# Loading an attention gradient's keys and query gradients already turned, by transposing DMAs

## The chip, the cores and the metric

The kernel runs on one core of a Trainium2 chip. The metric is device time in microseconds, as the median of several runs. The engines are called as the profile calls them: PE is TensorE (PEld its weight loads), DVE is VectorE, ACT is ScalarE, POOL is GpSimd, SP is SyncE, which issues the DMAs.

## The reference

Four residual layers over x of 2048 tokens by 512 features (bf16), each on a layer norm of x: attention, gated feed-forward, attention, gated feed-forward. The outputs are the result and, by `jax.vjp`, the gradients of x and of the five weights. The attention is linear, with 32 heads of 16:

```python
qkv = (x @ wqkv).reshape(B, S, 3, H, Dh)                     # q, k, v per head
phi = lambda t: jnp.where(t > 0, t + 1, jnp.exp(t)) + 1e-6
pq, pk = phi(q), phi(k)
kv = jnp.einsum("bhsd,bhse->bhde", pk, v)
z = jnp.einsum("bhsd->bhd", pk)
num = jnp.einsum("bhqd,bhde->bhqe", pq, kv)
den = jnp.einsum("bhqd,bhd->bhq", pq, z)[..., None] + 1e-6
o = num / den                                                # then @ wo
```

What matters here is the derivative of phi for the keys: for a positive key it is 1, for another exp(k), which is phi(k) - 1e-6. So the factor is min(pk - 1e-6, 1), and it can be made from the saved pk alone.

## The kernel before

Tokens are worked in 16 tiles of 128 (`NST`), features in four chunks of 128 (`NDC`). A forward pass over the four layers saves what the gradients need in DRAM (among it `pk`, the keys after phi, and `hT`, the normed input, turned). Then the gradient runs backwards over the layers: feed-forward 3, attention 2, feed-forward 1, attention 0. Weight gradients are sums over all tokens; they are computed by generators whose units (16 matmuls at line 1620, one PSUM bank, one evacuation) are put between the steps of other work: `next(fill)` issues one unit.

The gradient of an attention layer (class `ABwd`) has two parts. `first` computes the query gradients `dq` for all tokens, stores them in DRAM in two halves of 256 columns (`GW`), and computes the 512x512 product `GT`. `second`, the part that changes, runs over pairs of tiles (`NB2` = 2):

- `load(st)` loads a pair's `pk`, `dq`, `hT` and `h`, tokens on partitions; the first pair is loaded earlier, in `loaders`, into the tiles `pk_f`, `dq_f`, `hT_f`, `h_f`. All these DMAs are issued from SP, which issues one after another; a scheduler of the framework sets SP's order, while the orders of PE, DVE, ACT and POOL are as the program writes them (`manual_schedule`).
- `turn` transposes one tile's four chunks of `pk` and four of `dq` on PE into a PSUM bank (line 1869); ACT copies them to `pdT` (line 1870), and DVE makes the derivative factor `dphk` (line 1871).
- `keys` computes a pair's key gradients, turned: 16 matmuls into two banks (line 1881), and four DVE operations that add `dzc`, multiply by `dphk` and write `dkT` (line 1887).
- `finish` computes one tile's gradient of the normed input: 12 matmuls into one bank, four with `dq`, four with `pk`, the last four with `dkT` (line 1902). `LnAdd` then takes the layer norm's gradient: ACT makes a sum and, as a by-product that nobody reads, a copy into `dq_f` (line 1209); DVE makes a second sum and adds to x (lines 1210, 1211); POOL scales the two sums (line 1213). `end`, called a step later, makes the correction on ACT (line 1217) and adds it on POOL (line 1218). Its scratch is one of the first pair's tiles.
- `turn_keys` transposes four tiles of `dkT` in 32x32 blocks on DVE (line 989) and stores them; it runs for every second pair.

Before the loop stand the products of the layer (`ch_ps`), with two units of weight gradients between them. In the loop, a pair's `keys` come one pair ahead of its `finish`. PE's order in the loop for a pair is: turn, finish (even tile of the pair before), turn, keys, finish (odd tile of the pair before). PSUM has eight banks: "t", "g" and "u" with two each, "y" and "ln" with one each.

Of the kernel before, what the change touches and what calls it, by code (L numbers as in the profile page):

```python
# [9 lines left out]
BF16 = mybir.dt.bfloat16  # L10
F32 = mybir.dt.float32
ACT = mybir.ActivationFunctionType
ALU = mybir.AluOpType
# [5 lines left out]
D = 512  # L19
# [3 lines left out]
P = 128  # L23
NST = S // P
NDC = D // P
# [5 lines left out]
EPS = 1e-6  # L31
NB = 4
GW = 256
# [27 lines left out]
def ps_tile(k, which, shape, dt, name):  # L61
    return k.ps[which].tile(shape, dt, name=name, tag="ln_tp" if which == "ln" else f"{which}_ps")
# [318 lines left out]
def batch_rows(b, nb=NB):  # L381
    return slice(b * nb * P, (b + 1) * nb * P)


def dram_batch(ap2d, b, nb=NB):
    return ap2d[batch_rows(b, nb), :].rearrange("(n p) d -> p n d", p=P)
# [1262 lines left out]
class ABwd:  # L1649
# [161 lines left out]

    def loaders(self, fst):
        self.fst = {}
        self.fst["pk"] = fst.tile([P, 2, D], BF16, name="pk_f")
        self.fst["dq"] = fst.tile([P, 2, D], BF16, name="dq_f")
        self.fst["hT"] = fst.tile([P, 2, D], BF16, name="hT_f")
        self.fst["h"] = fst.tile([P, 2, D], BF16, name="h_f")
        for nm in ("pk", "dq", "hT", "h"):
            self.load_pair(nm, 0, self.fst[nm])

    def load_pair(self, nm, b, t):
        k, sv = self.k, self.k.sv[self.l]
        parts = [(t[:], sv[nm])]
        if nm == "dq":
            parts = [(t[:, :, g * GW:(g + 1) * GW], sv["dq"][g, :, :]) for g in range(D // GW)]
        for dst, src in parts:
            self.last_load = k.nc.sync.dma_start(out=dst, in_=dram_batch(src, b, 2)).ins

    def second(self, fill):
        k, l, small, ctx = self.k, self.l, self.small, self.ctx  # L1830
        nc, tc = k.nc, k.tc
        sv, NB2 = k.sv[l], 2
# [3 lines left out]
        Mv = late.tile([P, NDC, D], BF16, name="Mv")  # L1836
        with tc.tile_pool(name=f"ab_stg2{l}", bufs=2, reuse_waits="tile") as stg, \
# [7 lines left out]
            def load(st):  # L1845
                for nm in ("pk", "dq", "hT", "h"):
                    if st == 0:
                        cur[nm] = self.fst[nm]
                    else:
                        cur[nm] = stg.tile([P, NB2, D], BF16, name=f"{nm}_ld")  # L1850
                        self.load_pair(nm, st // NB2, cur[nm])
                with tc.issue_after(self.last_load):
                    if st == 6:
                        next(self.weights)
                    for b in (st - 2, st - 1):
                        if l == 2 and 0 <= b < NB:
                            k.load_a2(b)
                        if l == 0 and 0 <= b - 5 < NB:
                            k.load_h1(b - 5)
                return work.tile([P, NB2, NDC, P], BF16, name="dphk", bufs=1)  # L1860

            def turn(st, dphk):
                j = st % NB2
                T = dict(st=st, h=cur["h"][:, j, :])
                pdT = T["pdT"] = work.tile([P, 2, NDC, P], BF16, name="pdT", bufs=3)
                tps = ps_tile(k, "t", [P, 2, NDC, P], BF16, "T2_ps")
                for a, nm in enumerate(("pk", "dq")):
                    for c in range(NDC):
                        nc.tensor.transpose(tps[:, a, c, :], cur[nm][:, j, c * P:(c + 1) * P], k.ident[:])  # L1869
                nc.scalar.copy(pdT[:], tps[:])  # L1870
                nc.vector.tensor_scalar(dphk[:, j, :, :], pdT[:, 0, :, :], -EPS, 1.0, ALU.add, ALU.min)
                return T

            def keys(st, dphk):
                o = st % NB * P
                for half in range(2):
                    ps = ps_tile(k, "gu"[half], [P, 2, NB2 * P], F32, "dpk_ps")
                    for q in range(2):
                        c = 2 * half + q
                        for ic in range(NDC):  # L1880
                            nc.tensor.matmul(ps[:, q, :], lhsT=Nv[:, ic, c * P:(c + 1) * P],  # L1881
                                             rhs=cur["hT"][:, :, ic * P:(ic + 1) * P],
                                             start=(ic == 0), stop=(ic == NDC - 1))
                    for q in range(2):
                        c = 2 * half + q
                        tok = lambda t: t.rearrange("p (n t) -> p n t", n=NB2)
                        nc.vector.scalar_tensor_tensor(tok(dkT[:, c, o:o + NB2 * P]), tok(ps[:, q, :]), dzc[:, c:c + 1],
                                                       dphk[:, :, c, :], ALU.add, ALU.mult)

            def turn_keys(B):  # L1890
                for g in range(D // GW):
# [2 lines left out]
            def finish(T):  # L1894
                st = T["st"]
                dh_ps = ps_tile(k, ("y", "ln")[st % 2], [P, D], F32, "dh_ps")
                o = st % NB * P
                ops = [(T["pdT"][:, 1, c, :], k.wqkvT[:, c, :]) for c in range(NDC)]
                ops += [(T["pdT"][:, 0, c, :], Mv[:, c, :]) for c in range(NDC)]
                ops += [(dkT[:, c, o:o + P], k.wqkvT[:, NDC + c, :]) for c in range(NDC)]  # L1900
                for i, (lhsT, rhs) in enumerate(ops):
                    nc.tensor.matmul(dh_ps[:], lhsT=lhsT, rhs=rhs, start=(i == 0), stop=(i == len(ops) - 1))  # L1902
                spare = (self.fst[("pk", "hT")[st % 2]][:].rearrange("p n d -> p (n d)").bitcast(F32), self.fst["dq"][:, 0, :])
                ln = LnAdd(k, work, small, spare, dh_ps[:], T["h"], k.rstd[l][:, st:st + 1], k.xs[st])

                def end():
                    if self.out is None:
                        ln.end(k.xs[st][:])
                        return
                    out_t = outs[st // NB2 % 2]  # L1910
                    ln.end(out_t[:, st % NB2, :])
                    if st % NB2 == NB2 - 1:
                        nc.sync.dma_start(out=dram_batch(self.out, st // NB2, NB2), in_=out_t[:])
                return end

            dphk = load(0)
            Ts = [turn(j, dphk) for j in range(NB2)]
            dkv_ps = ps_tile(k, "g", [P, NDC, P], F32, "ch_ps")
            for c in range(NDC):
                cs = slice(c * P, (c + 1) * P)  # L1920
# [13 lines left out]
            for c in range(NDC):  # L1934
                ps = ps_tile(k, ("g", "y", "u", "ln")[c], [P, D], F32, "ch_ps")
                nc.tensor.matmul(ps[:], lhsT=dkvbdT[:, c, :], rhs=k.wqkvT[:, 2 * NDC + c, :], start=True, stop=True)
                evac_copy(k, Mv[:, c, :], ps[:], "vector" if c % 2 else "scalar")
            keys(0, dphk)
            prev, end = Ts, None
            for st in range(NB2, NST + NB2, NB2):  # L1940
                more, Ts = st < NST, []
                if more:
                    dphk = load(st)
                if not more:
                    end()
                    ends = [finish(T) for T in prev]
                    turn_keys(st // NB - 1)
                    for e in ends:
                        e()
                    break  # L1950
                for j in range(NB2):
                    Ts.append(turn(st + j, dphk))
                    if end is not None:
                        end()
                    if j:
                        keys(st, dphk)
                    end = finish(prev[j])
                if st % NB == NB2:
                    turn_keys(st // NB)
                prev = Ts  # L1960
# [10 lines left out]
def a_small_transposes(k, l, pool, GT, X_ld, dkvbdT):  # L1971
    nc = k.nc
    kvbdT = k.kv[l]["kvbdT"]
    T = {nm: pool.tile([P, NDC, w], BF16, name=nm) for nm, w in SMALL}
    jobs = [(T["G"][:, c, :], [GT[:, i, c * P:(c + 1) * P] for i in range(NDC)]) for c in range(NDC)]
    jobs += [(T["XT"][:, c, :], [X_ld[:, i, c * P:(c + 1) * P] for i in range(NDC)]) for c in range(NDC)]
    jobs += [(T["kvbd"][:].rearrange("p c f -> p (c f)"), [kvbdT[:, c, :] for c in range(NDC)]),
             (T["dkvbd"][:].rearrange("p c f -> p (c f)"), [dkvbdT[:, c, :] for c in range(NDC)])]
    for n, (dst, blocks) in enumerate(jobs):
        ps = ps_tile(k, "tg"[n % 2], [P, NDC, P], BF16, "fin_ps")  # L1980
        for i, b in enumerate(blocks):
            nc.tensor.transpose(ps[:, i, :], b, k.ident[:])
        evac_copy(k, dst, ps[:].rearrange("p c f -> p (c f)"), "vector" if n % 2 else "scalar")
    for nm, w in SMALL:
        nc.sync.dma_start(out=k.sv[l][nm].rearrange("(c p) j -> p c j", p=P), in_=T[nm][:])
# [58 lines left out]
```

## Time and profile before

| | |
|---|---|
| median of 3 runs | 1147.23 us (1147.04 to 1147.66) |
| the profiled execution | 1145.95 us, its span 1144.0 us |
| `second` of layer 2, first transpose to last `finish` | 599.4 to 669.9 us of the span |
| `second` of layer 0 | 935.9 to 1006.4 us of the span |
| DMA of the whole kernel | 258.18 MB, mean 226 GB/s |

The profile is one execution as the hardware profiler recorded it. Busy times are per engine; matmuls are pipelined and their ends modelled, so that the pitch from one to the next says more than the duration of one. Lines are those of the kernel file; a helper's operations all carry the helper's line.

### The profile page before, as it was taken

Reading aid. Unit: us, or ns where it says so; the run is one execution under the profiler, and the core shown is the slowest. Engines: PE = TensorE matmul, PEld = TensorE weight load, DVE = VectorE, ACT = ScalarE, POOL = GpSimd, SP = SyncE. Lnnn points to the kernel's source line nnn. Section 1 sums busy time; section 2 is a strip of 40 time slices with the busy share of each in tenths; the row PEclk is TensorE's granted clock in tenths of the full one; section 3 lists DMA queues with packets and bytes.
Section 4 is the critical chain, followed back from the end, with each engine's and each line's share of the span. In section 5 each row is a group of like instructions: output and inputs, shape, how many; then the busy total and the mean of one; then the engine's idle time right before and its main releaser. Section 6 shows DMA issues by size and latency. Waiting matters only on the chain. (4 is left out here: it accounts for less than half of the span.)

```text
span 1144.0 us, 21399 instructions
## 1 busy us (share of the span) xinstructions
PE 1122.8 (98%) x8026; PEld 698.8 (61%) x8026; DVE 745.5 (65%) x1311; ACT 552.9 (48%) x998; POOL 468.8 (41%) x627
## 2 busy tenths in 40 slices
PE   7999999999999999999999999999999999999998
PEld 4467777447777754445756656544447756665577
DVE  7787887888777667777966750067778947752221
ACT  4676666557676534445635651235546525630001
POOL 4738776435765446773102420048771103410000
PEclk9999999999999999999999999999999999999999
DMA  7945566534557677976899549787767886779775
GB/s 227 315 157 158 176 192 204 186 130 131 187 164 226 211 261 243 299 231 228 232 279 329 176 138 301 267 302 236 230 197 243 264 279 220 237 228 324 235 217 166
DMA packets 287145, 258.18 MB, mean 226 GB/s; under 512 B 29184, under 2 KB 263616, under 8 KB 287040
## 3 DMA queue, kind: packets, MB, share of 16 engines
q1 hardware_dynamic: 287040, 256.82, 70.4%
q8 instruction: 62, 1.02, 0.4%
q14 instruction: 43, 0.35, 0.1%
HBM read 136.25 MB, written 120.52 MB: 224 GB/s over the span
## 5 line engine op out<-in xcount | busy, mean ns | idle before, releaser
L1620 PE MATMUL p_ps<-p_set,p_a 128*128 128x384 bf16 (+2 forms) x1792 | 264.7, 303 | 1.3 <-DMA p_set<-sv_hdd 0.7
L1620 PEld LDWEIGHTS <-p_a 128*128 128x128 bf16 x1792 | 168.4, 95 | 84.3 <-PE p_ps L1620 1.0
L1329 POOL TENSOR_TENSOR dd<-dhb,ssd 128x512 bf16<-128x512 bf16 x84 | 96.9, 1157 | 110.6 <-ACT dhb L1327 108.0
L1328 DVE TENSOR_TENSOR dd<-dhh_ps,ssd 128x512 bf16<-128x512 f32 x85 | 57.2, 678 | 121.3 <-ACT dhb L1327 119.9
L1353 PE MATMUL dh_ps<-wuT,dd 128*128 128x512 bf16 (+1 forms) x340 | 128.9, 379 | 0.0
L1353 PE MATMUL dh_ps<-wgT,dd 128*128 128x512 bf16 (+1 forms) x340 | 128.8, 379 | 0.0
L1038 POOL TENSOR_TENSOR ssd_t<-hhT,oms 128x512 bf16<-128x512 bf16 (+1 forms) x92 | 99.8, 1091 | 67.2 <-DVE hhT L1037 42.6
L1353 PEld LDWEIGHTS <-dd 128*128 128x128 bf16 x680 | 66.4, 98 | 79.6
L1327 ACT CAST dhb<-dhh_ps 128x512 bf16<-128x512 f32 x84 | 48.7, 589 | 99.8 <-PE dhh_ps L1321 89.7
L1635 DVE TENSOR_TENSOR dw_stg<-p_ps,dw_stg 128x384 bf16<-128x384 f32 (+2 forms) x76 | 32.1, 437 | 99.0 <-PE p_ps L1620 96.2
L1019 PE MATMUL g_ps<-hT,wg 128*128 128x256 bf16 (+1 forms) x792 | 92.7, 260 | 1.6 <-ACT hT L376 0.9
L1019 PE MATMUL u_ps<-hT,wu 128*128 128x256 bf16 (+1 forms) x792 | 92.7, 261 | 0.8 <-DVE hhT L1037 0.8
L980 DVE STREAM_TRANSPOSE tr_stg<-dd 128x768 f32<-128x768 f32 (+1 forms) x62 | 86.6, 1436 | 1.1
L1037 DVE TENSOR_TENSOR hhT<-u_ps,ssd_t 128x512 bf16<-128x512 f32 (+1 forms) x92 | 58.0, 634 | 40.9 <-ACT ssd_t L1035 32.5
L1053 PE MATMUL y_ps<-wd,hhT 128*128 128x512 bf16 (+1 forms) x352 | 80.9, 379 | 0.1
L1321 PE MATMUL dhh_ps<-gT,wdT 128*128 128x512 bf16 x308 | 77.9, 379 | 1.2 <-DVE dd L1328 0.7
L1019 PEld LDWEIGHTS <-wg 128*128 128x128 bf16 x792 | 68.9, 98 | 16.0 <-issue 1.8
L1035 ACT ACTIVATE ssd_t<-g_ps 128x512 bf16<-128x512 f32 (+1 forms) x92 | 52.0, 565 | 50.9 <-PE g_ps L1019 33.6
L1019 PEld LDWEIGHTS <-wu 128*128 128x128 bf16 x792 | 70.6, 98 | 8.2 <-issue 1.2
L1637 ACT CAST dw_stg<-p_ps 128x384 bf16<-128x384 f32 (+2 forms) x76 | 28.1, 386 | 83.0 <-PE p_ps L1620 82.8
L1321 PEld LDWEIGHTS <-wdT 128*128 128x128 bf16 x352 | 33.9, 98 | 41.6 <-issue 3.8
L464 POOL TENSOR_TENSOR rstd_all<-rstd_all,neghalf 128x1 f32<-128x1 f32 x64 | 38.1, 596 | 47.5 <-DVE rstd_all L463 42.9
(276 smaller groups left out, 2085.9 us busy)
## 6 DMA issues: line engine op xcount, KB each, us to landing
sv_hdd<-tr_stg SPq DMA_DIRECT2D x72, 384.0 KB, 4.5
p_set<-sv_hdd SPq DMA_DIRECT2D x18, 1536.0 KB, 6.9
sv_ssd<-ssd_t SPq DMA_DIRECT2D x74, 256.0 KB, 2.4
ssd<-sv_ssd SPq DMA_DIRECT2D x23, 768.0 KB, 5.1
h_ld<-sv_h SPq DMA_DIRECT2D x30, 256.0 KB, 4.1
sv_hdl<-tr_stg SPq DMA_DIRECT2D x24, 256.0 KB, 4.7
p_a<-sv_h SPq DMA_DIRECT2D x12, 512.0 KB, 6.0
p_set<-sv_hdl SPq DMA_DIRECT2D x24, 256.0 KB, 5.3
```

The source lines that it names most:

```text
L980: nc.vector.transpose(t[:, :, 0:n * P].bitcast(F32).rearrange("p q (a j) -> p q a j", a=2 * n), src.rearrange("p c x -> p (c x)").bitcast( ...
L1019: nc.tensor.matmul(ps[:, ci * n:(ci + 1) * n], lhsT=w_sb[:, kc, (c0 + ci) * P:(c0 + ci + 1) * P], rhs=hT[:, kc, (st % 2) * P:(st % 2) * P ...
L1035: nc.scalar.activation(ssd[:, :, 0, :], gv, ACT.Sigmoid)
L1037: nc.vector.tensor_tensor(hh, uv, ssd[:, :, 0, :], ALU.mult)
L1038: nc.gpsimd.tensor_tensor(ssd[:, :, 1, :], hh, oms, ALU.mult)
L1053: nc.tensor.matmul(y_ps[:], lhsT=h[0:r, fc, off:off + P], rhs=k.wd[0:r, fc, :], start=(fc == 0), stop=(fc == NFC - 1))
L1321: nc.tensor.matmul(ps[:], lhsT=k.wdT[:, jc, u * P:(u + 1) * P], rhs=self.gT[B][:, jc, :], start=(jc == 0), stop=(jc == NDC - 1))
L1327: nc.scalar.copy(dhb[:], ps[:])
L1328: nc.vector.tensor_tensor(self.dd[ng][:, 0, c, :], ps[:], self.ssd[ng][:, c, 0, :], ALU.mult)
L1329: nc.gpsimd.tensor_tensor(self.dd[ng][:, 1, c, :], dhb[:], self.ssd[ng][:, c, 1, :], ALU.mult)
L1353: nc.tensor.matmul(self.acc[j][:], lhsT=dd[0:r, a, c, j * P:(j + 1) * P], rhs=w[0:r, u, :], start=(u == 0 and a == 0), stop=(u == NFC - 1 ...
L1620: nc.tensor.matmul(ps[:, 0:w], lhsT=lhs[:, s, ic * P:(ic + 1) * P], rhs=rhs, start=(s == 0), stop=(s == NST - 1))
```

## The change

`load_pair` loads `pk` and `dq` by `dma_start_transpose`: one DMA for a pair's keys (256 tokens by 512 columns), two for its query gradients (256 by 256 each). They arrive with features on partitions, as `[P, NDC, 256]`, in three buffers instead of two. `turn` is gone, with its transposes, `pdT` and PSUM bank; `finish` takes its weights from the loaded tiles. `dphk` is made once for a pair, by POOL, at the head of `keys`. The by-product of line 1209 goes to a PSUM tile of bank "t" instead of `dq_f`, and the correction's scratch for tile 0 is `hT_f`. One more unit of weight gradients stands ahead of the layer's products (the total is the same), and the transposes at the end of the layer take their banks in the other order.

```diff
     def loaders(self, fst):
         self.fst = {}
-        self.fst["pk"] = fst.tile([P, 2, D], BF16, name="pk_f")
-        self.fst["dq"] = fst.tile([P, 2, D], BF16, name="dq_f")
+        for nm in ("pk", "dq"):
+            self.fst[nm] = fst.tile([P, NDC, 2 * P], BF16, name=f"{nm}T_f")
...
     def load_pair(self, nm, b, t):
         k, sv = self.k, self.k.sv[self.l]
-        parts = [(t[:], sv[nm])]
-        if nm == "dq":
-            parts = [(t[:, :, g * GW:(g + 1) * GW], sv["dq"][g, :, :]) for g in range(D // GW)]
-        for dst, src in parts:
-            self.last_load = k.nc.sync.dma_start(out=dst, in_=dram_batch(src, b, 2)).ins
+        pair = batch_rows(b, 2)
+        if nm == "pk":
+            ins = k.nc.sync.dma_start_transpose(out=t[:], in_=sv["pk"][pair, :])
+        elif nm == "dq":
+            for g in range(D // GW):
+                n = GW // P
+                ins = k.nc.sync.dma_start_transpose(out=t[:, g * n:(g + 1) * n, :], in_=sv["dq"][g, pair, :])
+        else:
+            ins = k.nc.sync.dma_start(out=t[:], in_=dram_batch(sv[nm], b, 2))
+        self.last_load = ins.ins
...
-                        cur[nm] = stg.tile([P, NB2, D], BF16, name=f"{nm}_ld")
+                        if nm in ("pk", "dq"):
+                            cur[nm] = stg.tile([P, NDC, NB2 * P], BF16, name=f"{nm}T_ld", bufs=3)
+                        else:
+                            cur[nm] = stg.tile([P, NB2, D], BF16, name=f"{nm}_ld")
...
-            def turn(st, dphk):
-                j = st % NB2
-                T = dict(st=st, h=cur["h"][:, j, :])
-                pdT = T["pdT"] = work.tile([P, 2, NDC, P], BF16, name="pdT", bufs=3)
-                tps = ps_tile(k, "t", [P, 2, NDC, P], BF16, "T2_ps")
-                for a, nm in enumerate(("pk", "dq")):
-                    for c in range(NDC):
-                        nc.tensor.transpose(tps[:, a, c, :], cur[nm][:, j, c * P:(c + 1) * P], k.ident[:])
-                nc.scalar.copy(pdT[:], tps[:])
-                nc.vector.tensor_scalar(dphk[:, j, :, :], pdT[:, 0, :, :], -EPS, 1.0, ALU.add, ALU.min)
-                return T
...
-            def keys(st, dphk):
+            def keys(st):
                 o = st % NB * P
+                dphk = work.tile([P, NDC, NB2 * P], BF16, name="dphk", bufs=1)
+                nc.gpsimd.tensor_scalar(dphk[:], cur["pk"][:], -EPS, 1.0, ALU.add, ALU.min)
...
-                ops = [(T["pdT"][:, 1, c, :], k.wqkvT[:, c, :]) for c in range(NDC)]
-                ops += [(T["pdT"][:, 0, c, :], Mv[:, c, :]) for c in range(NDC)]
+                ops = [(T["dq"][:, c, :], k.wqkvT[:, c, :]) for c in range(NDC)]
+                ops += [(T["pk"][:, c, :], Mv[:, c, :]) for c in range(NDC)]
...
-                spare = (self.fst[("pk", "hT")[st % 2]][:].rearrange("p n d -> p (n d)").bitcast(F32), self.fst["dq"][:, 0, :])
+                r = self.fst["hT" if st == 0 or st % 2 else "pk"][:].rearrange("p n d -> p (n d)").bitcast(F32)
+                spare = (r, ps_tile(k, "t", [P, D], F32, "t_junk")[:])
...
-            dphk = load(0)
-            Ts = [turn(j, dphk) for j in range(NB2)]
+            prev = load(0)
+            next(fill)
...
                 for j in range(NB2):
-                    Ts.append(turn(st + j, dphk))
                     if end is not None:
                         end()
                     if j:
-                        keys(st, dphk)
+                        keys(st)
                     end = finish(prev[j])
```

More of the change, by code (lines that the diff above doesn't have):

```diff
@@ L1859, in load @@
                             k.load_h1(b - 5)
-                return work.tile([P, NB2, NDC, P], BF16, name="dphk", bufs=1)
-            def turn(st, dphk):
-                j = st % NB2
-                T = dict(st=st, h=cur["h"][:, j, :])
-                pdT = T["pdT"] = work.tile([P, 2, NDC, P], BF16, name="pdT", bufs=3)
-                tps = ps_tile(k, "t", [P, 2, NDC, P], BF16, "T2_ps")
-                for a, nm in enumerate(("pk", "dq")):
-                    for c in range(NDC):
-                        nc.tensor.transpose(tps[:, a, c, :], cur[nm][:, j, c * P:(c + 1) * P], k.ident[:])
-                nc.scalar.copy(pdT[:], tps[:])
-                nc.vector.tensor_scalar(dphk[:, j, :, :], pdT[:, 0, :, :], -EPS, 1.0, ALU.add, ALU.min)
-                return T
-            def keys(st, dphk):
+                return [dict(st=st + j, h=cur["h"][:, j, :], pk=cur["pk"][:, :, j * P:(j + 1) * P],
+                             dq=cur["dq"][:, :, j * P:(j + 1) * P]) for j in range(NB2)]
+            def keys(st):
                 o = st % NB * P
+                dphk = work.tile([P, NDC, NB2 * P], BF16, name="dphk", bufs=1)
+                nc.gpsimd.tensor_scalar(dphk[:], cur["pk"][:], -EPS, 1.0, ALU.add, ALU.min)
                 for half in range(2):
@@ L1885, in keys @@
                         c = 2 * half + q
-                        tok = lambda t: t.rearrange("p (n t) -> p n t", n=NB2)
-                        nc.vector.scalar_tensor_tensor(tok(dkT[:, c, o:o + NB2 * P]), tok(ps[:, q, :]), dzc[:, c:c + 1],
-                                                       dphk[:, :, c, :], ALU.add, ALU.mult)
+                        nc.vector.scalar_tensor_tensor(dkT[:, c, o:o + NB2 * P], ps[:, q, :], dzc[:, c:c + 1],
+                                                       dphk[:, c, :], ALU.add, ALU.mult)
             def turn_keys(B):
@@ L1937, in second @@
                 evac_copy(k, Mv[:, c, :], ps[:], "vector" if c % 2 else "scalar")
-            keys(0, dphk)
-            prev, end = Ts, None
+            keys(0)
+            end = None
             for st in range(NB2, NST + NB2, NB2):
[L1941 to L1944, printed above, removed]
+                if st < NST:
+                    Ts = load(st)
+                else:
                     end()
@@ L1979, in a_small_transposes @@
     for n, (dst, blocks) in enumerate(jobs):
-        ps = ps_tile(k, "tg"[n % 2], [P, NDC, P], BF16, "fin_ps")
+        ps = ps_tile(k, "gt"[n % 2], [P, NDC, P], BF16, "fin_ps")
         for i, b in enumerate(blocks):
```

## The prediction

> **What bounds the kernel now.** First the page's busy table, then the two stages that the change touches (function `second`, once per attention layer, found by the first and last starts of lines 1869 and 1902), by the view of windows.
>
> ```profile
> PE 1122.8 (98%) x8026; PEld 698.8 (61%) x8026; DVE 745.5 (65%) x1311; ACT 552.9 (48%) x998; POOL 468.8 (41%) x627
> 599.40:669.90 70.50, 70.50 (x517) 43.67 (x516) 48.26 (x106) 41.03 (x67) 23.10 (x43) 1.00 0.68 216
> 935.90:1006.40 70.50, 70.50 (x520) 43.67 (x518) 49.36 (x108) 40.27 (x65) 23.15 (x44) 1.00 0.70 219
> ```
>
> Columns of the last two: window, its length, busy of PE, PEld, DVE, ACT, POOL, granted clock, DMA share, GB/s. TensorE is never idle in either 70.5 us, at full clock. The chain that ended last, in order of time, shows how one pair of tiles is paced (start, duration, what):
>
> ```profile
> 973.43 1.75 PE dpk_ps L1881 x16
> 975.18 2.59 PE dh_ps L1902 x12
> 977.77 0.45 PE T_ps L1869 x8
> 978.22 2.59 PE dh_ps L1902 x12
> 980.80 0.45 PE T_ps L1869 x8
> 981.25 1.75 PE dpk_ps L1881 x16
> ```
>
> A pair takes 7.82 us of pure TensorE: two `finish` (2.59 each), one `keys` (1.75), two turns (0.45 each). So the stage is TensorE's, and what leaves TensorE shortens it only if no chain through other engines is as long. The timeline shows that chain (start, duration, engine, line, names):
>
> ```profile
> 980.90 0.69 ACT L1209 ACTIVATE dq_f<-dh_ps,rstd_all 128x512 bf16<-128x512 f32 x1 [0.27 <-PE dh_ps L1902]
> 981.49 0.19 ACT L1209 ACTIVATION_READ_ACCUMULATOR dq_f<-dh_ps,rstd_all 128x1 f32 x1
> 981.77 0.75 DVE L1210 SCALAR_TENSOR_TENSOR junk<-dh_ps,rstd_all,h_ld 128x512 bf16<-128x512 f32 x1 [1.40 <-issue]
> 982.61 0.19 POOL L1213 TENSOR_SCALAR ab<-c 128x1 f32<-128x1 f32 x1 [0.48 <-DVE junk L1210]
> 982.84 0.81 ACT L1217 ACTIVATE pk_f<-h_ld,ab,ab 128x512 f32<-128x512 bf16 x1 [0.25 <-POOL ab L1213]
> 983.11 0.28 DVE L1871 TENSOR_SCALAR dphk<-pdT 128x512 bf16<-128x512 bf16 x1
> 983.50 1.66 DVE L1887 SCALAR_TENSOR_TENSOR dkT<-dpk_ps,dzc,dphk 128x256 bf16<-128x256 f32 x4
> 983.74 1.27 POOL L1218 TENSOR_TENSOR out_t<-x,pk_f 128x512 bf16<-128x512 f32 x1 [0.93 <-ACT pk_f L1217]
> ```
>
> The even tile's layer-norm end runs ACT, DVE, POOL, ACT, POOL and is finished at 985.01. Today nothing on TensorE needs it: `dphk` is made on DVE (983.11), `dkT` starts at 983.50. That POOL takes its instructions strictly in turn can be seen a tile later, in POOL's own timeline:
>
> ```profile
> 988.53 1.28 POOL L1218 TENSOR_TENSOR out_t<-x,hT_f 128x512 bf16<-128x512 f32 x1 [0.93 <-ACT hT_f L1217]
> 989.78 0.19 POOL L1213 TENSOR_SCALAR ab<-c 128x1 f32<-128x1 f32 x1
> 990.94 0.19 POOL L1213 TENSOR_SCALAR ab<-c 128x1 f32<-128x1 f32 x1 [0.96 <-DVE junk L1210]
> ```
>
> The first L1213 of the even tile had its operand at 989.50 (ACT's read of the sum ended) and started only when the odd tile's add was over.
>
> **Removed from TensorE.** 16 tiles x 8 transposes x 2 layers = 256. Eight take 0.446 us (980.80 to 981.25), so 14.3 us, all on the path. ACT loses 32 evacuations (L1870, 1.00 us each), DVE 32 `dphk` (L1871, 0.28): neither set the pace. Alone this gives 6.93 us a pair.
>
> **The step that decides: `dphk` on POOL.** POOL executes in order. In the changed program its order for a pair is: two L1213 and the add L1218 of the odd tile before, two L1213 and L1218 of the even tile, then `dphk`. So `dphk`, which needs only the loaded keys, waits for the even tile's add, and the four `dkT` operations (L1887, now 1886) wait for `dphk`; behind these on DVE stand the odd tile's L1210 and L1211, and TensorE's next `finish` needs `dkT` for its last four matmuls. That `finish` feeds the next L1209: a ring through all four engines. One lap, from the end of `dkT`:
> - DVE does the odd tile's L1210 at once (+0.05). From the start of an L1210 to the end of its L1217 the rows above give 983.65 - 981.77 = 1.88 us. ACT holds the next even tile's L1209 behind that L1217, and L1209 to L1210 is 0.87, so the even L1210 starts at 0.05 + 1.88 + 0.87 = 2.80. TensorE is not last there: its fourth `dkT` matmul ends at about 0.3, ACT could start at 0.6.
> - L1210's start to L1218's end: 985.01 - 981.77 = 3.24, now 6.04.
> - `dphk`, 128x1024 on POOL: no such row, but the groups by line have its half, a two-operation tensor_scalar:
>
> ```profile
> L224 POOL TENSOR_SCALAR out_t<-x 128x512 bf16<-128x512 f32 x2 | 1.2, 620 | 2.1 <-DVE x L1055 2.1
> ```
>
>   Twice that less one start of about 0.09 is 1.15, now 7.19. Bounds: 0.62 (no growth with width) and 2.12 (the 128x1024 tensor_tensor of L891).
> - handover and four `dkT`: 0.05 + 1.66 = 1.71, the lap is **8.90**.
> - Every second pair the two key transposes (L989, 2.09 us) stand on DVE behind the odd L1211 (which ends at 1.48): the even L1210 starts at 3.57 and the lap is **9.67**.
>
> The mean is 9.29 against TensorE's 6.93: TensorE would stand idle 2.4 us a pair, where today it is never idle.
>
> **Sum for a layer**, from the first `finish` to the last: the first lap starts free, with `dkT` ready at 2.59 + 1.13 (end of `finish` to L1210) + 3.24 + 1.15 + 1.71 = 9.8; six laps follow, three of each kind, 55.7; then the last `finish` waits for its PSUM bank (L1211 of the tile two before, 1.5 after `dkT`) and takes 2.59. That is 69.6. Today: 7 x 7.82 + 2 x 2.59 = 59.9. Less the first pair's 16 transposes (0.89): +8.8 a layer, **+17.6** for two. Each 0.1 us in a lap is worth 7 x 2 x 0.1 = 1.4, so `dphk` at its bounds gives +10 or +31.
>
> **The transposing loads.** No run here shows one. Each pair asks for three (keys 256 KB, query gradients 2 x 128 KB), three buffers deep instead of two; needed about two laps after issue. Lower bound: as the plain loads, which land in 4.5 us (keys) and 4.4 (gradients): hidden, 0; a gain is excluded, as no engine waits for a load in these stages today. For the work: queue 1 shows 287040 packets in 70.4% of 16 engines' span, 44.9 ns each. Plain, a pair has 256 key rows and 512 half rows, 768 packets; if a turned load moves 128 columns of a row at a time, 2048: 3.6 us more a pair on 16 engines. The stage's DMA work, 0.68 and 0.70 of 70.5, grows from 48 and 49 us to 73 and 74, in a stage that by the ring lasts 79: hidden, narrowly. I take 0, the same queue and bytes, and keep the upper bound as a rival. [...]
>
> **At nothing.** One unit of 16 filler matmuls (2.64 us) goes from the stage's end to its head: TensorE does it either way. It covers the first pair's loads, as do the chain products: `dqT_f` is first used some 12 us after the transposes of today (599.4); without that cover up to its 4.4 us. The sum's copy (L1209) goes to PSUM: between 0.59 (L1327, a cast of the same size) and 0.81 (L1217) for 0.69, which over 14 laps is 2 us either way. On SP the issues of a pair (980.66 to 988.47) take 3.3 us, the three now turned 1.5 of them; even at three times that SP is done in 6.3, below the lap. There the later loads change places (hT first, `h` behind the keys of the next pair but one, which wait for a free buffer); all are issued a lap or more ahead, and if one is late `finish` or L1210 waits for it. POOL's eight `dphk` a layer delay only L1213 and L1218, which the lap counts. The stage after gets its `x` as late as the ring ends, no more.
>
> The profiled execution took 1145.95 us (span 1144.0 and 1.95 around it); the median is 1147.23, 1.28 above. 1145.95 + 17.6 + 1.28 = **1164.8**.
>
> **Rivals.**
> 1. *The ring does not bind* (faster). For: POOL is only a third busy in the stage (23.1 of 70.5), and the transposes are on the path. The point from which it decides is a mean lap of 8.0 (9.29 less 8.8 / 7), where gain and ring cancel; at 6.93 or less the whole gain is left: 1147.2 - 14.3 = 1133. It could come if `dphk` and the handovers cost almost nothing. Against: `dphk` at 0.3 still leaves 8.4, and the other terms are rows of operations that stay, in the same order. Chance 0.08.
> 2. *The turned loads set the pace.* If only one is under way at a time, each at its plain landing time, a pair takes 4.5 + 2 x 4.4 = 13.3 us, more than the lap; seven pairs from the stage's start and some 9 us of work behind the last make 102 instead of 70.5: 2 x 31.5 more, 1210. For: by the packets above the DMA work has only 5 us of room a stage, and a turned packet may take longer than a plain one. Against: plain loads of this queue overlap freely, and the lap itself leaves each load some 18 us. Chance 0.17. [...]
> 3. *No difference*: laps near 8.0, gain and ring cancel, 1147. Chance 0.03.
>
> **How the numbers follow.** Forecast 0.72. The range 1153 to 1202 takes the forecast with `dphk` at either bound (1157 to 1179), 4 us below for handovers that are quicker than read, and on the other side part of rival 2, loads that lengthen each stage by up to 18 us more (1164.8 + 2 x 18.6); it leaves out rival 1, no difference, and the rest of rival 2. A measurement of this kernel can tell some 0.2% (2.3 us) from none: faster 0.08, same 0.03, slower 0.89.
>
> **What would show it.** In the changed trace: the stages last about 79 us, not 70.5; TensorE idles in them before the last four matmuls of the even `finish`, released by L1886; DVE waits at L1886 for POOL's `dphk`; POOL's row shows `dphk` at 1.15 directly behind L1218; starts of `dphk` 8.9 and 9.7 us apart in turn. I am wrong if TensorE stays full and a pair takes 6.93, or if POOL's `dphk` or TensorE's first group of `finish` waits for DMA, which is rival 2.

## The result, and the profile after

The changed kernel takes 1198.13 us (median of 5 runs, 1195.62 to 1200.46) against 1147.23 for the kernel before on the same chip (5 runs, 1147.04 to 1148.17): a ratio of 1.0443, interval 1.043 to 1.0455. That is 50.9 us slower, where 17.6 were forecast. The profiled execution took 1198.13 us, its span 1196.2.

The page's busy table, and the two stages by the view of windows. The columns are those of before: window, length, busy PE, PEld, DVE, ACT, POOL, granted clock, DMA share, GB/s. Each window starts with the moved filler unit (2.64 us) and ends with the last `finish`.

```profile
PE 1130.2 (94%) x7770; PEld 688.3 (58%) x7770; DVE 737.5 (62%) x1279; ACT 521.8 (44%) x966; POOL 527.5 (44%) x643
599.51:697.00 97.49, 77.23 (x415) 40.68 (x414) 44.17 (x90) 25.92 (x52) 48.52 (x50) 0.91 0.59 158
962.06:1060.63 98.57, 78.38 (x423) 41.37 (x422) 46.05 (x94) 25.27 (x50) 48.49 (x50) 0.91 0.66 163
```

PE has the 256 instructions fewer that were announced, yet it is idle for 20 us in each stage. POOL's busy time has doubled, from 23.1 to 48.5. The page's groups name the two waits, one behind the other:

```profile
L1901 PE MATMUL dh_ps<-wqkvT,dkT 128*128 128x512 bf16 x128 | 42.4, 427 | 39.6 <-DVE dkT L1886 39.6
L1886 DVE SCALAR_TENSOR_TENSOR dkT<-dpk_ps,dzc,dphk 128x256 bf16<-128x256 f32 x64 | 26.6, 477 | 78.1 <-POOL dphk L1875 77.8
```

PE waits 39.6 us for `dkT`; DVE, before `dkT`, waits 77.8 us for POOL's `dphk`. One lap of the ring in the timeline (start, duration, engine, line, names):

```profile
653.61 3.63 POOL L1875 TENSOR_SCALAR dphk<-pkT_ld 128x1024 bf16<-128x1024 bf16 x1
...
657.27 1.66 DVE L1886 SCALAR_TENSOR_TENSOR dkT<-dpk_ps,dzc,dphk 128x256 bf16<-128x256 f32 x4 [5.56 <-POOL dphk L1875]
...
657.81 1.89 PE L1901 MATMUL dh_ps<-wqkvT,dkT 128*128 128x512 bf16 x4 [4.16 <-DVE dkT L1886]
...
658.84 0.74 DVE L1210 SCALAR_TENSOR_TENSOR junk<-dh_ps,rstd_all,h_ld 128x512 bf16<-128x512 f32 x1
...
659.90 0.81 ACT L1217 ACTIVATE hT_f<-h_ld,ab,ab 128x512 f32<-128x512 bf16 x1 [7.07 <-POOL ab L1213]
660.62 0.64 ACT L1209 ACTIVATE t_junk<-dh_ps,rstd_all 128x512 f32<-128x512 f32 x1
...
661.42 0.75 DVE L1210 SCALAR_TENSOR_TENSOR junk<-dh_ps,rstd_all,h_ld 128x512 bf16<-128x512 f32 x1 [1.16 <-ACT t_junk L1209]
...
662.49 0.81 ACT L1217 ACTIVATE pkT_f<-h_ld,ab,ab 128x512 f32<-128x512 bf16 x1 [1.10 <-POOL ab L1213]
...
663.38 1.26 POOL L1218 TENSOR_TENSOR x<-x,pkT_f 128x512 f32<-128x512 f32 x1 [0.93 <-ACT pkT_f L1217]
...
664.73 3.63 POOL L1875 TENSOR_SCALAR dphk<-pkT_ld 128x1024 bf16<-128x1024 bf16 x1
```

This is the ring that the prediction drew, operation for operation: `dphk`, `dkT`, the odd tile's L1210 and L1217, the even tile's L1209, L1210, L1217 and L1218, then the next `dphk`. Each starts within 0.1 us of the end of the one before it, but for two small steps between them: ACT's read of its sum behind L1209, and POOL's L1213 between an L1210 and its L1217. The starts of `dphk` in this stage lie 11.13 and 11.87 us apart in turn (641.73, 653.61, 664.73, 676.59, 687.71). The new thing is the first line: `dphk` takes 3.63 us. The lines of one source show that it always does (number, then min/median/max in ns), and how the turned loads stand:

```profile
L1875 POOL TENSOR_SCALAR dphk<-pkT_ld x14: 3626/3626/3643, 618.7 to 1051.3; 128x1024 bf16<-128x1024 bf16 x14
L1826 SPq DMA_TRANSPOSE pkT_ld<-sv_pk x14: 1226/1252/7255, 598.7 to 1028.2; - x14
L1830 SPq DMA_TRANSPOSE dqT_ld<-sv_dq x28: 1188/1264/2622, 602.1 to 1030.7; - x28
```

A turned load keeps SP for about 1.25 us (the median; the longest took 7.3). No engine waits for one in the loop. Only ahead of the loop does POOL's first `dphk` of a layer wait for a DMA: 6.0 us for the first pair's keys (`pkT_f`, at 952.8, layer 0), and 5.7 us in layer 2, which the profile puts down to the store of `dq`; nothing was late for either.

Where the 52.2 us of span (1196.2 less 1144.0) are: from the first chain product (L1922) to the start of the last four `dkT` matmuls a stage took 68.75 and 68.74 us before and takes 93.99 and 95.07 now, which is +51.6; the first pairs' transposes are gone (-1.8); and PE waits 3.1 us instead of 0.7 for `p_set` at 726.92, behind layer 2's stage (+2.4).

### The profile page after: what moved, and what is told of

The parts are those of the page before. It is cut to its first block, busy times and chain, and to the rows that moved or that the text cites. A ratio compares the mean times of both kernels' runs of the same rounds, so it can differ in the third digit from the quotient of the medians.

```text
span 1196.2 us, 20805 instructions
## 1 busy us (share of the span) xinstructions
PE 1130.2 (94%) x7770; PEld 688.3 (58%) x7770; DVE 737.5 (62%) x1279; ACT 521.8 (44%) x966; POOL 527.5 (44%) x643
## 5 line engine op out<-in xcount | busy, mean ns | idle before, releaser
L1901 PE MATMUL dh_ps<-wqkvT,dkT 128*128 128x512 bf16 x128 | 42.4, 427 | 39.6 <-DVE dkT L1886 39.6
L1886 DVE SCALAR_TENSOR_TENSOR dkT<-dpk_ps,dzc,dphk 128x256 bf16<-128x256 f32 x64 | 26.6, 477 | 78.1 <-POOL dphk L1875 77.8
```

## The experiments

The theory (A, where the expectations use letters): the ring sets the pace, because `dphk` is queued on POOL behind the even tile's add, and its length is the operation's own. Rivals: the turned loads share in the loss; `dphk` is slow only beside other work; the moved unit costs something. The runs are counted here in the order in which they are told. Intervals below are those of the ratio to the kernel before, run on the same chip (medians 1147.13 to 1147.86).

**1. The factor on DVE, nothing else undone.**

```diff
-                nc.gpsimd.tensor_scalar(dphk[:], cur["pk"][:], -EPS, 1.0, ALU.add, ALU.min)
+                nc.vector.tensor_scalar(dphk[:], cur["pk"][:], -EPS, 1.0, ALU.add, ALU.min)
```

> The changed kernel with its derivative factor on DVE (same place in the program, same 128x1024 operation), so that only the turned loads are left of the change. Theory (the ring through POOL's dphk costs all, the turned loads nothing): the ring is broken, a pair takes TensorE's 6.93 us, 1147.2 - 14.3 = 1133, TensorE without idle time in the two stages; dphk about 0.49 us on DVE (L662 of before, 128x1024). Rival (the turned loads pace the stages): TensorE or DVE waits for pkT_ld or dqT_ld, the time stays above 1147. Second rival (turned loads cost other transfers their time): stages at 6.93 a pair, but stalls elsewhere, 1135 to 1147.

Measured: 1147.16 us (1142.14 to 1149.24, 12 runs), ratio 0.9995 (0.9983 to 1.0007). All of the loss is gone, and with it the waits for `dkT`; but the 1133 that the theory gave is missed, and of the gain nothing is left. PE's waits and the place of the longest in PE's timeline:

```profile
PE dpk_ps L1881 <- DMA hT_ld<-sv_hT: 5.1, 1, 5.1
PE p_ps L1620 <- DMA p_set<-sv_hdd: 3.1, 2, 2.7
```
```profile
990.74 3.57 PE L1881 MATMUL dpk_ps<-hT_ld,X_Nv 128*128 128x256 bf16 x16 [5.09 <-DMA hT_ld<-sv_hT]
994.11 1.83 PE L1901 MATMUL dh_ps<-wqkvT,dqT_ld 128*128 128x512 bf16 x4
```

In layer 0's stage PE stands 5.09 us for a plainly loaded tile, `hT`, and the matmuls behind it run at half pace (16 in 3.57 us, 1.91 elsewhere). SP's own timeline shows what went just ahead of it:

```profile
985.26 1.28 SPq L1830 DMA_TRANSPOSE dqT_ld<-sv_dq  x1
986.59 0.57 SPq L1832 DMA_DIRECT2D hT_ld<-sv_hT  x1
987.26 1.36 SPq L1826 DMA_TRANSPOSE pkT_ld<-sv_pk  x1
988.67 2.57 SPq L1830 DMA_TRANSPOSE dqT_ld<-sv_dq  x2
```

SP issues almost without a pause, and `hT` was issued at 986.59 behind the turned loads; 4.1 us later it is there. In layer 2, where no load is late, the stage is 62.49 us in the measure above: the 68.75 of before less 14 tiles x 0.446. So the saving on PE is real. The accounts of this span (1145.1): -14.3 as forecast, +8.8 in layer 0's stage (71.30 instead of 62.5), +3.9 between the stages, +2.4 ahead of the first (1.7 of it before any line that was changed), +0.4 behind.

**2. The same place on POOL, a cheap pair of operators.** The minimum is left out.

```diff
-                nc.gpsimd.tensor_scalar(dphk[:], cur["pk"][:], -EPS, 1.0, ALU.add, ALU.min)
+                nc.gpsimd.tensor_scalar(dphk[:], cur["pk"][:], 1.0, 0.0, ALU.mult, ALU.add)
```

> The changed kernel with POOL's operation of the same size and place, but a multiply by 1 and an add of 0 in place of the add and the min; it leaves the minimum out, so the factor is wrong where a key is over 1. Theory A (the minimum is what makes POOL's operation take 3.63 us instead of 1.15): it takes about 1.15, laps of 8.9 and 9.7 us, and the time is the forecast's sum, 1165. Theory B (bf16 source, or the width): it stays at 3.6 us, and the time at 1198. Between the two, each 0.1 us of the operation should be worth 14 laps x 0.1 = 1.4 us.

Measured: 1159.51 us (1158.18 to 1160.72), ratio 1.0099 (1.0083 to 1.0115). The line's durations, and PE's wait:

```profile
L1875 POOL TENSOR_SCALAR dphk<-pkT_ld x14: 1044/1044/1047, 619.1 to 1018.0; 128x1024 bf16<-128x1024 bf16 x14
```
```profile
PE dh_ps L1901 <- DVE dkT L1886: 12.6, 11, 1.5
```

Same ring, same place, 1.044 us instead of 3.626: laps of 8.42 and 9.15, and 38.6 us less. That is 15.0 us for each us of `dphk`; the prediction had 14. It is 5.5 us below the 1165 that was expected: `dphk` is 0.1 us shorter than the forecast's 1.15, and the laps are another 0.4 shorter than its sum.

**3. What the operation costs by itself.** POOL operations on their own data, behind the end of the changed kernel; the whole program's time (1234.15 us, one run) is of no use here.

```diff
+        for _ in range(2):
+            g(ob[:], sb[:], -EPS, 1.0, ALU.add, ALU.min)
+            g(ob[:, 0:D], sb[:, 0:D], -EPS, 1.0, ALU.add, ALU.min)
+            g(ob[:, 0:D], sf[:, 0:D], -EPS, 1.0, ALU.add, ALU.min)
...
+            g(ob[:], sb[:], 1.0, 0.0, ALU.mult, ALU.add)
...
+            g(ob[:], sb[:], -EPS, 1.0, ALU.add, ALU.add)
+            g(ob[:], sb[:], -EPS, 1.0, ALU.add, ALU.mult)
...
+            g(ob[:], sb[:], 1.0, None, ALU.min)
```

> The changed kernel followed, behind its last work, by POOL operations on scratch tiles, one form a line (its longer time means nothing). Theory A (the minimum): add then min takes 3.63 us at 1024 columns and about 1.9 at 512, whatever the source's type; mult then add, add then add and add then mult take about 1.15 at 1024; add then max is as slow as min. Theory B (a bf16 source): mult then add of bf16 is slow too, add then min of an f32 source takes 0.62 at 512. Theory C (contention in the stage): add then min takes about 1.15 here, where nothing else runs.

POOL's timeline, in the order of the diff (L343 add and min; L344 and L345 half as wide, from bf16 and from f32; L347 mult and add; L350 add and add; L351 add and mult; L354 min alone):

```profile
1069.70 3.63 POOL L343 TENSOR_SCALAR pb_ob<-pb_bf 128x1024 bf16<-128x1024 bf16 x1 [1.69 <-DMA out_dram<-h_f]
...
1075.40 1.92 POOL L344 TENSOR_SCALAR pb_ob<-pb_bf 128x512 bf16<-128x512 bf16 x1
...
1079.40 1.92 POOL L345 TENSOR_SCALAR pb_ob<-pb_f 128x512 bf16<-128x512 f32 x1
1081.40 1.04 POOL L347 TENSOR_SCALAR pb_ob<-pb_bf 128x1024 bf16<-128x1024 bf16 x1
...
1083.93 3.64 POOL L350 TENSOR_SCALAR pb_ob<-pb_bf 128x1024 bf16<-128x1024 bf16 x1
1087.65 1.04 POOL L351 TENSOR_SCALAR pb_ob<-pb_bf 128x1024 bf16<-128x1024 bf16 x1
...
1092.51 3.63 POOL L353 TENSOR_SCALAR pb_ob<-pb_bf 128x1024 bf16<-128x1024 bf16 x1
1096.22 2.78 POOL L354 TENSOR_SCALAR pb_ob<-pb_bf 128x1024 bf16<-128x1024 bf16 x1
...
1101.06 3.63 POOL L343 TENSOR_SCALAR pb_ob<-pb_bf 128x1024 bf16<-128x1024 bf16 x1
```

In the first round the last weight gradients still run on TensorE beside the operations; in the second, at 1101.06, PE, DVE and ACT stand idle and SP issues no DMA (1098 to 1128 us), and the operation takes the same 3.63 us. So it is not slowed by other work. Nor is it the type of the source: bf16 and f32 both take 1.92 for 512 columns. It is the operators: mult with add, in either order, takes 1.04; add with min, with max (L353) or with another add, and mult with min (L352, 3.65), take 3.63 to 3.65; min alone lies between, at 2.78. That add with add is among the slow ones was not expected: the name of one operator does not tell it. Why these pairs are slow no run here shows. DVE makes the same add and min in 0.43 (L357 of this run; 0.42 to 0.43 at L1875 of run 1).

**4. The factor on POOL, but at the head of the step**, ahead of the odd tile's add, so that the ring is cut without touching the operation: once a pair, before the loop over its two tiles.

```diff
+            def factor():
+                dphk = work.tile([P, NDC, NB2 * P], BF16, name="dphk", bufs=2)
+                nc.gpsimd.tensor_scalar(dphk[:], cur["pk"][:], -EPS, 1.0, ALU.add, ALU.min)
+                return dphk
...
+                    dphk = factor()
...
-                        keys(st)
+                        keys(st, dphk)
```

> The changed kernel with POOL's dphk issued at the head of the pair's step, ahead of the odd tile's add, into two buffers; nothing else moves. Theory (its place behind the even tile's add makes the ring): dkT no longer waits for the even add, the ring is gone, and POOL's own work per pair is the next bound: 3.63 + 2 x 1.27 + 4 x 0.2 = 7.0 us, just over TensorE's 6.93, so 7.0 to 7.6 a pair, 1134 to 1143. Rival (a POOL operation of 3.63 us costs its length wherever it stands): still above 1185.

Measured: 1156.67 us (1154.82 to 1158.48), ratio 1.0078 (1.0062 to 1.0093) and so slower than was expected. The ring is gone: inside a stage the starts of `dphk` are an even 7.93 us apart, not 11.5. But now POOL sets the lap. Its work of a pair was expected to take 7.0 us; one wait of 0.93 us for ACT's L1217 comes on top, as the odd tile's add and the even tile's L1213 stand behind the 3.63 of `dphk`. PE waits elsewhere:

```profile
PE dpk_ps L1884 <- DMA hT_ld<-sv_hT: 6.3, 2, 6.1
PE dh_ps L1904 <- DVE x L1211: 5.2, 5, 2.5
```

The second line is a PSUM bank that DVE frees late; the first is a late `hT`, as in run 1. Moving the order costs less than the ring, and still more than DVE.

**5. The ring without the turned loads**: the kernel before, with only the factor given to POOL, two of 128x512 a pair at the head of `keys`.

```diff
-                nc.vector.tensor_scalar(dphk[:, j, :, :], pdT[:, 0, :, :], -EPS, 1.0, ALU.add, ALU.min)
+                T["dphk"] = dphk[:, j, :, :]
...
-            def keys(st, dphk):
+            def keys(st, dphk, Ts):
+                for T in Ts:
+                    nc.gpsimd.tensor_scalar(T["dphk"], T["pdT"][:, 0, :, :], -EPS, 1.0, ALU.add, ALU.min)
...
```

> The kernel before with only the factor moved to POOL, at the head of keys, one 128x512 operation a tile (two a pair, 1.92 us each by the probe); loads and TensorE's transposes as before. Theory (the ring alone makes the loss, the turned loads no part of it): the laps of the changed kernel with 2 x 1.92 = 3.84 instead of 3.63, and up to 0.9 us of ACT's copies in a lap, TensorE's transposes in its idle time: 7 x (11.6 to 12.6) a layer, 1199 to 1215. Rival (the changed kernel lost half of its 51 us by the turned loads): 1165 to 1185.

Measured: 1203.01 us (1201.66 to 1205.2), ratio 1.0485 (1.047 to 1.0501).

```profile
L1877 POOL TENSOR_SCALAR dphk<-pdT x32: 1917/1918/1932, 601.6 to 1054.8; 128x512 bf16<-128x512 bf16 x32
```
```profile
PE dh_ps L1904 <- DVE dkT L1889: 32.6, 14, 3.6
```

Plain loads, transposes on PE, and the loss is there whole: laps of 11.37 and 12.13, 0.25 more than in the changed kernel, as two halves take 3.84 and not 3.63. The factor on POOL alone makes the loss; the turned loads have no part in it that can be seen in the laps.

**6. The turned loads alone**: the factor on DVE as in run 1, and plain loads in place of the turned ones, so that nothing is transposed at all.

```diff
-            ins = k.nc.sync.dma_start_transpose(out=t[:], in_=sv["pk"][pair, :])
+            ins = k.nc.sync.dma_start(out=t[:].rearrange("p c t -> p (c t)").rearrange("p (n d) -> p n d", n=2), in_=dram_batch(sv["pk"], b, 2))
...
-                ins = k.nc.sync.dma_start_transpose(out=t[:, g * n:(g + 1) * n, :], in_=sv["dq"][g, pair, :])
+                ins = k.nc.sync.dma_start(out=t[:, g * n:(g + 1) * n, :], in_=dram_batch(sv["dq"][g, :, :], b, 2))
```

> The kernel with the factor on DVE, its turned loads replaced by plain loads of the same bytes into the same tiles, with nothing turned anywhere (so the gradients of this part come out of unturned data). Theory (the turned loads themselves cost what TensorE saved, through SP's issues and the DMA engines): without them the stages run at 6.93 us a pair with no wait for a load, and the time is 1147.2 - 14.3 = 1133, up to 1137 with the stall for a weight-gradient set behind layer 2's stage. Rival (the saving was lost for another reason, such as the moved filler unit or shorter stages that meet the set loads): it stays at 1143 to 1148.

Measured: 1138.31 us (1136.35 to 1139.22), ratio 0.9917 (0.9904 to 0.9931): 8.9 us better than run 1 by the medians, and a little above the 1133 to 1137 that were expected. The price of turning shows in the DMA view of 600 to 670 us, first of this run, then of run 1:

```profile
DMA packets 17866, 15.55 MB, mean 222 GB/s; under 512 B 848, under 2 KB 16323, under 8 KB 17859
q1 hardware_dynamic: 17859, 15.46, 69.0%
```
```profile
DMA packets 28017, 16.25 MB, mean 232 GB/s; under 512 B 15722, under 2 KB 26474, under 8 KB 28010
q1 hardware_dynamic: 28010, 16.16, 91.1%
```

For about the same bytes there are some 14900 more small packets, 2100 for each of the seven pairs, and 22% more of 70 us of all DMA engines, 2.2 us a pair. They land little later (3.7 us plain, 4.0 to 4.6 turned). That SP's time is what gets scarce is argued from run 1's SP timeline and tried in run 7. Turning is not the whole cause, though: here too, with plain loads, PE waits once for a late `hT` in layer 0,

```profile
PE dpk_ps L1881 <- DMA hT_ld<-sv_hT: 1.2, 1, 1.2
```

and that stage takes 65.00 us, layer 2's 62.49.

**7. Turned loads kept, the late one mended**: run 1 with `hT` and `h` issued first and in three buffers.

```diff
-                for nm in ("pk", "dq", "hT", "h"):
+                for nm in ("hT", "h", "pk", "dq"):
...
-                            cur[nm] = stg.tile([P, NB2, D], BF16, name=f"{nm}_ld")
+                            cur[nm] = stg.tile([P, NB2, D], BF16, name=f"{nm}_ld", bufs=3)
```

> The kernel with the factor on DVE, hT and h asked for ahead of the turned loads and three buffers deep. Theory (in layer 0 a plain load of hT was late because it stood on SP behind turned loads): the 5.1 us wait for hT_ld in layer 0's stage goes, and with it the slow matmuls behind it (1.7), so about 1140. Rival (DMA and SP are simply full in layer 0's stage, whatever the order): another load is late in its place, pkT_ld or dqT_ld, and the time stays at 1145 to 1148.

Measured: 1136.75 us (1134.7 to 1140.3), ratio 0.9909 (0.9892 to 0.9927): 1% better than the kernel before, and with run 9 the fastest of all runs here. In layer 0 the stage is 63.62 instead of run 1's 71.30, in layer 2 63.07. The order and the third buffer were changed together, so the run does not say which of the two mends it. A busy queue alone does not make `hT` late: its share is 94.6% here over 600 to 670 us, where the longest wait for `hT` is 0.43 us, and 88.4% in run 1 over 930 to 1010, where PE waits 5.09. Most of what is left of the loss lies between the stages, at PE's first wait behind layer 2's:

```profile
697.52 6.76 PE L1620 MATMUL p_ps<-p_set,p_a 128*128 128x384 bf16 x30 [2.50 <-DMA p_set<-sv_hdd]
```

It was 0.73 before. Run 6, with plain loads, has it too (3.26 at 698.33), so it does not come from turning. Run 9 bears on where it comes from.

**8. Only the keys turned by DMA**, query gradients on PE as before, factor on DVE.

```diff
-                ins = k.nc.sync.dma_start_transpose(out=t[:, g * n:(g + 1) * n, :], in_=sv["dq"][g, pair, :])
+                ins = k.nc.sync.dma_start(out=t[:, :, g * GW:(g + 1) * GW], in_=dram_batch(sv["dq"][g, :, :], b, 2))
...
+            def turn(T):
+                T["dq"] = work.tile([P, NDC, P], BF16, name="dqT", bufs=4)
+                tps = ps_tile(k, "t", [P, NDC, P], BF16, "T2_ps")
+                for c in range(NDC):
+                    nc.tensor.transpose(tps[:, c, :], T["dq_ld"][:, c * P:(c + 1) * P], k.ident[:])
+                nc.scalar.copy(T["dq"][:], tps[:])
```

> Only the keys are loaded turned (one DMA a pair, 1024 short packets); the query gradients are loaded plainly and turned on TensorE, four transposes a tile, copied by ACT; factor on DVE. Half of TensorE's saving, 7.1 us. Theory (SP and DMA are full only where both are turned): a pair takes 7.38 us, no late loads in layer 0, 1140. Rival (every turned load costs what it saves): 1147. Should the whole fall below the kernel before and below the factor on DVE alone, it is the better version.

Measured: 1142.74 us (1142.26 to 1145.05), ratio 0.9963 (0.995 to 0.9977). Half of the transposes gone (7.15 us) bring 5.1, without any change to the order of the loads: with one turned load a pair in place of three, PE waits 0.16 us at most for an `hT`.

**9. The moved unit put back**: run 7 without the unit ahead of the chain products.

```diff
             prev = load(0)
-            next(fill)
```

> The kernel of e6 (factor on DVE, hT and h asked for first, three deep) with the moved unit of 16 weight-gradient matmuls back behind the stage, as in the kernel before. Theory (the unit's place costs nothing, and the stall of 2.5 us on a weight-gradient set behind layer 2's stage comes of DMA engines that are full there): the same time within 2 us, 1135 to 1139, the stall behind the stage still there. Rival (the moved unit makes the stall, or it covers the first pair's loads): 1133 if the stall goes, 1141 or more if TensorE waits for pkT_f or dqT_f at the head of the stages.

Measured: 1137.03 us (1136.33 to 1139.54), ratio 0.991 (0.9896 to 0.9923), beside 1136.75 for run 7: its place costs nothing that can be measured in the total. Within the trace it does shift waits. The one for `p_set` behind layer 2's stage is 1.24 us instead of 2.50, and so it sorts over the runs: 2.1 to 3.3 us in seven traces with the unit moved (the changed kernel and runs 1, 2, 4 and 6 to 8), 0.7 to 1.4 in the three without (the kernel before, runs 5 and 9). With one unit less behind the stage, PE comes sooner to the matmuls that need the next set. In exchange, in this trace of run 9 PE waits 3.24 us at 987.57 in layer 0 for a PSUM bank, released by DVE's L1211.

## Why the prediction was right and wrong

- **The direction and the mechanism held.** The ring runs through the operations that were named, PE's wait is at the four `dkT` matmuls of the even `finish`, and DVE stands at L1886 for `dphk`. Run 5 makes the loss with the factor on POOL alone, run 1 takes it away by the engine alone.
- **The step that failed is `dphk` at 1.15 us, "twice that less one start".** It takes 3.63, outside both bounds (0.62 and 2.12). The row taken, L224 at 620 ns, is a two-operation tensor_scalar of half the width but of other operators, mult with add; for that pair 1.15 was nearly right (1.04 in run 2). The 0.09 of a start was the author's estimate, and no run shows it as the fixed part of an operation: mult with add at 512 and 1024 columns in run 3 (0.617 at L348, 1.044 at L347) gives 0.19. Both tensor_scalars of 512 columns that POOL has in the kernel before (L224 and L655) are mult with add, so none of its rows held the price of add with min. With 3.63 in the prediction's own sum, the change is 17.6 + 14 x (3.63 - 1.15) = 52.3 and the time 1199.5; 1198.13 was measured. The upper bound was no bound: the tensor_tensor of the same width takes 2.12, and add with min 3.63, 3.5 times as long as mult with add (1.04).
- **Two hits are luck.** The range, 1153 to 1202, holds 1198.13 only by the room that it left for slower loads; for `dphk` it ended at 1179 (by its own terms 1178.4), and no load took the room. And that 1199.5 lies so near is in part two errors that nearly cancel: the laps, read too long, are worth 3.6 us, and the wait for `p_set` behind layer 2's stage, where the prediction has nothing, 2.4.
- **The handovers were read 0.26 us a lap too long.** With 3.63 the laps would have been 11.38 and 12.15; they were 11.13 and 11.87. In the lap shown, from the end of `dkT` to the even tile's L1210 it is 2.49, not 2.80: the odd L1210 and the even L1209 each start 0.09 before the operation ahead of them on the engine has ended, and L1209 to L1210 is 0.80, not 0.87. Starting `dphk` and `dkT` gives 0.1 back. This is the smaller part, and it goes the other way.
- **The turned loads at 0 held in the changed kernel**, where the slow laps hide them. Rival 2 did not come: turned loads of the same queue are issued some 1.25 us apart and land 3.4 to 3.5 us after issue (600 to 670 us of the changed kernel; `hT`, plain, lands in 3.8 there), so they overlap. Run 7, which turns by DMA, is 1% quicker than the kernel before, which turns on TensorE. The packets (2048 estimated a pair) are there, some 2100 small ones, at 2.2 us a pair instead of 3.6. But the 0 rested on the ring: once it is gone, a load that stands on SP behind the turned ones comes late, and run 1 loses 8.8 us in layer 0 (run 6, with plain loads, 2.5). That part of the prediction, three times the issue time on SP and later loads that change places, was seen as possible and priced only for the long lap.
- **Rival 1, "1147.2 - 14.3 = 1133", was the right size for PE.** Without the ring the layer 2 stage shortens by just the transposes of its 14 tiles. Of the whole, run 7 keeps 11.1.
- **The work at nothing** held for the first pair's loads, and for the unit in the total (run 9). For the work behind layer 2's stage it did not hold, by the 2.4 us of `p_set`: the moved unit shows there, though it does not explain all of it, as run 5 and run 9 still wait 1.4 and 1.2, not 0.7.

## What to carry to other kernels

Take an operation's duration on an engine from a row with the same operators, not only the same shape: here two tensor_scalars of one shape differ by 3.5 times, and each us of it cost 15 on the path (run 2). An engine that is a third busy (POOL: 23.1 of 70.5 us) can still be a poor place for an operation that stands between two engines in a ring of handovers: here `dphk` needs only the loaded keys, is queued in program order behind the add that the ring makes late, and starts 0.09 us after that add ends (664.73); run 5, with nothing else moved, took 55 us more than the kernel before. Work that a slow stage hides, here the issue time of turned loads (1.25 us each on SP), has to be priced again for the stage as it would be once it is quick.

## What the runs showed of the hardware

- POOL's tensor_scalar goes by its operators (run 3, 128 partitions, 1024 columns of bf16): 1.04 us for mult with add in either order, 2.78 for min alone, 3.63 to 3.65 for add with min, max or add and for mult with min. That is 1.0 to 3.6 ns a column.
- After a wait PE may run slower than before it, and the length of the wait does not settle it. In the changed kernel the clock is full after a wait of 1.65 us and half after one of 4.16 (the windows of 646 to 652 and 657.8 to 663.1); run 6 waits 3.26 us and goes on at 1.00, run 7 waits 2.50 and has a mean of 0.60 in the 4 us shown (698 to 702 in both; run 6 first).

```profile
646.00:652.00 6.00, 5.99 (x34) 3.19 (x35) 5.71 (x11) 2.13 (x4) 1.83 (x4) 1.00 0.33 95
657.80:663.10 5.30, 5.29 (x21) 3.12 (x22) 3.88 (x9) 2.09 (x4) 1.81 (x4) 0.50 0.19 54
```
```profile
698.00:702.00 4.00, 3.67 (x23) 2.17 (x24) 0.00 (x0) 0.48 (x1) 0.00 (x0) 1.00 1.02 368
```
```profile
698.00:702.00 4.00, 4.00 (x17) 1.93 (x15) 0.00 (x0) 0.28 (x1) 0.00 (x0) 0.60 1.05 370
```

  In the ring this costs little: the four slowed `dkT` matmuls end at 659.70, still ahead of ACT's L1209 at 660.62. In run 1, where PE sets the pace, the 16 matmuls behind the late `hT` took 1.7 us more.
- A transposing DMA of 128 to 256 KB keeps SP for 1.25 us to issue, by the medians of the changed kernel (a plain load of 256 KB 0.37 and 0.58), though it lands about as soon (3.4 to 3.5 us, plain 2.7 and 3.8, in 600 to 670).
